# A GELU MLP's forward and backward on one core: part of the gate's arithmetic moved to GpSimd, and the first loads in another order

## The chip, the cores and the metric

One core of a Trainium2 chip runs the whole program. The metric is its device time in microseconds; three runs of the kernel before took 275.57, 275.65 and 275.70 us. Engines are named as in the profile: PE multiplies matrices, DVE, ACT and POOL (GpSimd) work element by element, SP issues DMAs, as ACT and POOL do too.

## The reference

```
h   = gelu(x @ w1 + b1)          # tanh form; x: 2048 x 448, w1: 448 x 1792
out = h @ w2 + b2                # w2: 1792 x 448
grads of x, w1, b1, w2, b2 from grad_out (2048 x 448)
```

All tensors are bf16. With v = x @ w1 + b1 the backward pass needs gelu'(v) times q, where q = grad_out @ w2 transposed; that product, gh, gives the gradients of x, w1 and b1, and h with grad_out gives that of w2.

## The kernel before, in words

The 2048 rows are four blocks of 512, the 1792 features seven pairs of 128-wide tiles, so there are 28 steps g (block, pair), and features lie on the partitions. The order of every engine's work is the order of the source: the schedule is written by hand, and each engine runs its own instructions in that order, waiting on the others where data demand it.

What a step computes, for a tile pair of 128 x 1024:

- PE: `M1` (L218) multiplies w1 with x into PSUM tile u, six matmuls of depth 128; `rest` (L229) adds the two of depth 64 and opens q with its own two; `M4` (L242) finishes q with six. u and q have one PSUM buffer each.
- ACT, `act_first` (L248): two rows copy u plus b1 into V (f32, the L252 rows), a Square with a scale gives A (L253), Gelu gives h (L254). `act_second` (L271): tanh of Bt into t (L272).
- DVE, `dve_first` (L268): Bt = (A + 3c) * V, the cubic. `dve_second` (L275): p = (A + c) * h, the slope (L276); t + 1 (L277); p - 0.5 (L278); t = t * p (L279). `dve_gate` (L281): gh = (t + 1) * q, with q read from PSUM.

V, A and Bt have one buffer each, t and p two each, in turn by the parity of the step.

The main loop (L373 to L416) does, for step g: `rest` for u of step g + 1 and q of step g, `M4(g)`, the gate of g, `act_first` and `dve_first` of g + 1, tanh and `dve_second` of g + 1, then "pieces", matmuls of output rows: those of h with w2 give out (o-pieces; in steps 0 to 6 eight each, for feature tiles 2g and 2g + 1), those of gh with w1 transposed give the gradient of x. `M1(g + 2)` ends the step on PE. Step 0's first part is done ahead of the loop (L367 to L372), with four dummy matmuls inside step 0 (L381 to L384). At step 6 the pieces, with two matmuls that add b2, and two copies on ACT stand ahead of tanh.

Loads are issued ahead of the loop, nearly all on SP's queue (L170 to L205), plain ones for w1 (`load_w1`, by feature columns) and w2 (`load_w2`, by feature tiles), transposing ones for x, grad_out (`load_x`, `load_g`; gq is the transposed grad_out of a block), w2 and w1 (`load_w2T`, `load_w1T`; each w2T load is two DMAs, L155 and L156). A DMA waits for the landing of the DMA eight places before it, and for what its target's data demand. A matmul that reads a part of w2 waits for the load that last wrote that part.

After step 27 come the rest of the pieces and the gradients of w1 and w2 (L430 to L499), all on PE, with sums for b1 and b2 on DVE and POOL's all-reduce (L446, L457).

Of the kernel before, what the change touches and what calls it, by code (L numbers as in the profile page):

```python
# [8 lines left out]
ACT = mybir.ActivationFunctionType  # L9
ALU = mybir.AluOpType  # L10
# [4 lines left out]
GELU_C = math.sqrt(2.0 / math.pi)  # L15
# [3 lines left out]
def kernel(  # L19
# [15 lines left out]
    nc = tc.nc  # L35
    P = 128
    B, S, D = x.shape
    F = w1.shape[1]
    assert B == 1
    NS = S // P  # L40
    NF = F // P
# [8 lines left out]
    NPAIR = NF // 2  # L50
# [33 lines left out]
    T_flat = const.tile([P, 4 * 2 * SB], BF16, name="T")  # L84
# [4 lines left out]
    w1_sb = w1_flat.rearrange("p (k f) -> p k f", k=KD)  # L89
# [9 lines left out]
    def xq(b):  # L99
        o = (b % 2) * 2 * KD * SB  # L100
        return xg_flat[:, o:o + KD * SB].rearrange("p (k s) -> p k s", k=KD)
# [5 lines left out]
    def ring(t, n, g):  # L107
        o = (g % n) * 2 * SB
        return t[:, o:o + 2 * SB].rearrange("p (h s) -> p h s", h=2)

    def hT(g):
        return ring(hT_flat, HR, g)
# [4 lines left out]
    def V_of(g):  # L117
        return VA_flat[:, 0:2 * SB].rearrange("p (h s) -> p h s", h=2)

    def A_of(g):  # L120
        return VA_flat[:, 2 * SB:4 * SB].rearrange("p (h s) -> p h s", h=2)

    def B_of(g):
        return ring(B_flat, 1, g)

    def t_of(g):
        return ring(T_flat, 4, 2 * (g % 2))

    def p_of(g):
        return ring(T_flat, 4, 2 * (g % 2) + 1)  # L130

    ctx.enter_context(tc.manual_schedule())

# [3 lines left out]
    def load_x(b):  # L137
        rows = slice(b * SB, (b + 1) * SB)
        nc.sync.dma_start_transpose(out=xq(b)[:, 0:KF, :], in_=x2[rows, DL:D])
        nc.sync.dma_start_transpose(out=xq(b)[:, KF, :], in_=x2[rows, 0:P])  # L140
# [6 lines left out]
    def load_w1(eng, f0, f1):  # L147
        eng.dma_start(out=w1_sb[:, 0:KF, f0:f1], in_=w1[DL:D, f0:f1].rearrange("(k p) f -> p k f", p=P))
        eng.dma_start(out=w1_sb[0:DL, KF, f0:f1], in_=w1[0:DL, f0:f1])

    def load_w2(eng, t0, t1):
        eng.dma_start(out=w2_sb[:, t0:t1, :], in_=w2[t0 * P:t1 * P, :].rearrange("(t p) d -> p t d", p=P))

    def load_w2T(f0, f1):
        nc.sync.dma_start_transpose(out=w2T_sb[:, KF, f0:f1], in_=w2[f0:f1, DOV:D])  # L155
        nc.sync.dma_start_transpose(out=w2T_sb[:, 0:KF, f0:f1], in_=w2[f0:f1, 0:DM])  # L156
# [21 lines left out]
    pw = psum_a.tile([P, SB], F32, name="acc")  # L178
# [8 lines left out]
        nc.tensor.matmul(pw[:], lhsT=warm[:, 0:P], rhs=warm, start=True, stop=True)  # L187
    load_w2T(256, 512)
    load_w2(nc.sync, 2, 4)
    load_w1(nc.sync, 768, 1280)  # L190
    load_w2T(512, 768)
    load_w2(nc.sync, 4, 8)
    load_w2T(768, 1024)
    load_w1(nc.sync, 1280, F)
    load_w2T(1024, 1280)
    load_w2(nc.sync, 8, NF)
    load_w2T(1280, 1536)
# [10 lines left out]
    def blk(g):  # L208
        return divmod(g, NPAIR)

    def cols(g, h):
        c = g % NPAIR
        return slice((2 * c + h) * P, (2 * c + h + 1) * P)
# [4 lines left out]
    def M1(g):  # L218
        if g == 0:
            u_of[g] = [psum_a.tile([P, SB], F32, name="acc")[:] for h in range(2)]  # L220
        else:
            u = psum_u.tile([P, 2, SB], F32, name="u")
            u_of[g] = [u[:, h, :] for h in range(2)]
        for h in range(2):
            for kt in range(KF):
                nc.tensor.matmul(u_of[g][h], lhsT=w1_sb[:, kt, cols(g, h)], rhs=xq(g // NPAIR)[:, kt, :],  # L226
                                 start=(kt == 0), stop=False, skip_group_check=True)

    def rest(gu, gg):  # L229

        if gg is not None:
            q = psum_g.tile([P, 2, SB], F32, name="q")
            g_of[gg] = q
        for h in range(2):
            if gu is not None:
                nc.tensor.matmul(u_of[gu][h], lhsT=w1_sb[0:DL, KF, cols(gu, h)], rhs=xq(gu // NPAIR)[0:DL, KF, :],  # L236
                                 start=False, stop=True, tile_position=(0, 0), skip_group_check=True)
            if gg is not None:
                nc.tensor.matmul(q[:, h, :], lhsT=w2T_sb[DL:P, KF, cols(gg, h)], rhs=gq(gg // NPAIR)[DL:P, KF, :],
                                 start=True, stop=False, tile_position=(DL, 0), skip_group_check=True)  # L240

    def M4(g):  # L242
        for h in range(2):
            for kt in range(KF):
                nc.tensor.matmul(g_of[g][:, h, :], lhsT=w2T_sb[:, kt, cols(g, h)], rhs=gq(g // NPAIR)[:, kt, :],  # L245
                                 start=False, stop=(kt == KF - 1), skip_group_check=True)

    def act_first(g):  # L248
        u = u_of.pop(g)
        for h in range(2):  # L250
            ft = 2 * (g % NPAIR) + h
            nc.scalar.activation(out=V_of(g)[:, h, :], in_=u[h], func=ACT.Identity, bias=b1_col[:, ft:ft + 1])  # L252
        nc.scalar.activation(out=A_of(g), in_=V_of(g), func=ACT.Square, scale=math.sqrt(3.0 * GELU_C * GELU_A))  # L253
        nc.scalar.activation(out=hT(g), in_=V_of(g), func=ACT.Gelu_apprx_tanh)  # L254

    def first_step(g):
# [8 lines left out]
                                           in1=V_of(g)[:, h, :], op0=ALU.add, op1=ALU.mult)  # L265
        nc.scalar.activation(out=hT(g), in_=V_of(g), func=ACT.Gelu_apprx_tanh)  # L266

    def dve_first(g):  # L268
        nc.vector.scalar_tensor_tensor(out=B_of(g), in0=A_of(g), scalar=3.0 * GELU_C, in1=V_of(g), op0=ALU.add, op1=ALU.mult)  # L269

    def act_second(g):  # L271
        nc.scalar.activation(out=t_of(g), in_=B_of(g), func=ACT.Tanh, scale=-1.0 / 3.0)  # L272


    def dve_second(g):  # L275
        nc.vector.scalar_tensor_tensor(out=p_of(g), in0=A_of(g), scalar=GELU_C, in1=hT(g), op0=ALU.add, op1=ALU.mult)  # L276
        nc.vector.tensor_scalar(out=t_of(g), in0=t_of(g), scalar1=1.0, scalar2=None, op0=ALU.add)  # L277
        nc.vector.tensor_scalar(out=p_of(g), in0=p_of(g), scalar1=-0.5, scalar2=None, op0=ALU.add)  # L278
        nc.vector.tensor_tensor(out=t_of(g), in0=t_of(g), in1=p_of(g), op=ALU.mult)  # L279

    def dve_gate(g):  # L281
        nc.vector.scalar_tensor_tensor(out=ghT(g), in0=t_of(g), scalar=1.0, in1=g_of.pop(g)[:], op0=ALU.add, op1=ALU.mult)  # L282

    def store_h(g):
        b, c = blk(g)
        nc.gpsimd.dma_start(out=hT_dram_v[:, 2 * c:2 * c + 2, b * SB:(b + 1) * SB], in_=hT(g))  # L286
# [50 lines left out]
    def run_pieces(units):  # L337
        for un in units:
            if un.piece():
                full.append(un)  # L340

    def flush(by_act=None):
        for un in [un for un in full if by_act in (None, un.by_act)]:
            full.remove(un)
            evict(un)
# [22 lines left out]
    rest(0, None)  # L368
    first_step(0)
    act_second(0)  # L370
    dve_second(0)
    M1(1)  # L372
    for g in range(NSTEP):  # L373
        b, c = blk(g)
        pieces = [U[k] for k in seq[b] for _ in range(NF)]
        n = len(pieces)
        own = pieces[n * c // NPAIR:n * (c + 1) // NPAIR]
        grown = [U[k] for k in grow[b] for _ in range(2)]
        nxt = g + 1 if g + 1 < NSTEP else None
        rest(nxt, g)  # L380
        if g == 0:  # L381

            for i in range(4):
                nc.tensor.matmul(pw[:], lhsT=w1_sb[:, 0, 0:P], rhs=xq(0)[:, 0, :], start=True, stop=True)  # L384
        M4(g)
        flush(False)
        dve_gate(g)
        if nxt is not None:
            act_first(nxt)
        flush(True)  # L390
        if nxt is not None:
            dve_first(nxt)
        last = b == 0 and c == NPAIR - 1
        if last:
            run_pieces(grown + own)
            flush(True)
        if nxt is not None:
            act_second(nxt)
            dve_second(nxt)
        if g == NPAIR:  # L400
            run_pieces(grown)
            M1(g + 2)
            run_pieces(own)
        elif not last:
            run_pieces(grown + own)
        if g != NPAIR and g + 2 < NSTEP:
            M1(g + 2)
        for _ in range(2):
            if g >= NPAIR - 1 and stored < g:
                store_h(stored)  # L410
                stored += 1
        if c == 2 and 0 < b < NB - 1:
            load_x(b + 1)
            load_g(b + 1)
        for t in turns.get(g, []):
            turn_gh(*t)  # L416
# [45 lines left out]
    for t0, t1 in ((0, 4), (4, HT)):  # L462
        n = (t1 - t0) * P
        for h in range(2):
            a0, a1 = t0 + h * HT, t1 + h * HT
            cs = slice(a0 * P, a1 * P)
            for kt in range(KF):
                ps = psum_a.tile([P, SB], F32, name="acc")
                psv = ps[:, 0:n].rearrange("p (t f) -> p t f", f=P)
                for st in range(NS):  # L470
                    nc.tensor.matmul(psv, lhsT=x_all[:, st, kt * P:(kt + 1) * P], rhs=gh_rows(st, a0, a1),  # L471
                                     start=(st == 0), stop=(st == NS - 1))
# [3 lines left out]
        for st in range(NS):  # L476
            for h in range(2):
                psv = ps[h * DL:(h + 1) * DL, 0:n].rearrange("p (t f) -> p t f", f=P)
                nc.tensor.matmul(psv, lhsT=x_all[:, st, KF * P:D], rhs=gh_rows(st, t0 + h * HT, t1 + h * HT),  # L479
                                 start=(st == 0), stop=(st == NS - 1), tile_position=(0, h * DL), skip_group_check=True)  # L480
        nc.scalar.copy(out=gw1_rem[:, t0 * P:t1 * P], in_=ps[:, 0:n])
        for h in range(2):
            nc.scalar.dma_start(out=out_2[KF * P:D, (t0 + h * HT) * P:(t1 + h * HT) * P],
                                in_=gw1_rem[h * DL:(h + 1) * DL, t0 * P:t1 * P])
# [45 lines left out]
```

## Time and profile before

| what | us |
|---|---|
| median of three runs | 275.65 |
| the profiled execution | 275.59 |
| its span in the profile | 273.8 |
| PE busy | 267.6 |
| DVE busy | 189.3 |
| ACT busy | 143.7 |
| POOL busy | 54.6 |
| step 3 on PE, first matmul of q to that of step 4 | 4.75 |

The profile is of one execution. Its busy lines give each engine's time at work; matmuls overlap, so that one row is longer than the distance to the next. A row of the timeline reads: start, length, engine, line, operation, what it writes and reads, shape, and in brackets the idle time before it and what ended that. A row of the DMA view reads: tiles, issuing queue, size, and the time from issue to landing. A row of the waits reads: who waited, for whom, the total, how often, the longest. Between the span and the device time lie 1.8 us of start and end that no row shows.

### The profile page before, as it was taken

The page shows a single profiled execution, that of the slowest core. Times are in us where ns is not written, and L with a number is a line of the kernel's source. Part 1 is how long each engine was busy: PE and PEld are TensorE (multiplying, and loading weights), DVE is VectorE, ACT ScalarE, POOL GpSimd, SP SyncE. Part 2 cuts the span into 40 slices and gives each one's busy share as a digit, 9 for nine tenths or more (in the row PEclk, how much of TensorE's full clock was granted, in tenths as well). Part 3 has the DMA queues.
Part 4 walks back from the last instruction along what each step waited for, and adds up shares of the span by engine and source line. Part 5 has one row for each costly group of instructions (what it writes and reads, how often), then busy time and mean ns, then how long its engine had stood idle before and what let it go on. Part 6 is the DMA issues. An engine that isn't in the chain of part 4 may idle for free.

```text
span 273.8 us, 3596 instructions
## 1 busy us (share of the span) xinstructions
PE 267.6 (98%) x1406; PEld 123.7 (45%) x1406; DVE 189.3 (69%) x218; ACT 143.7 (52%) x188; POOL 54.6 (20%) x57
## 2 busy tenths in 40 slices
PE   7899999999999999999999999999999999999995
PEld 3343434443444344444444445554445655555552
DVE  0799999999999999999888871139999970000000
ACT  2878879788888778887777740011111221112111
POOL 6000002730301403033031135111700019400000
PEclk9999999999999999999999999999999999999999
DMA  7878979999999928055534339999999931101111
GB/s 164 172 190 193 213 117 170 274 317 246 199 242 203 249 58 163 24 154 122 138 113 79 110 105 217 325 335 241 165 201 273 225 100 57 44 9 50 50 51 35
DMA packets 101379, 43.78 MB, mean 160 GB/s; under 512 B 90353, under 2 KB 97905, under 8 KB 101362
## 3 DMA queue, kind: packets, MB, share of 16 engines
q1 hardware_dynamic: 94272, 26.68, 51.6%
q0 software_dynamic: 4544, 14.92, 16.9%
q10 hardware_dynamic: 2546, 1.95, 2.5%
q8 instruction: 11, 0.18, 0.3%
q14 instruction: 6, 0.05, 0.1%
HBM read 7.00 MB, written 14.23 MB: 78 GB/s over the span
## 4 chain that ended last, share of the span: by engine, by line
PE 82%; DVE 12%; ACT 2%; DMA 2%; issue 1%; DVEq 0%
PE acc L313 27%; PE acc L490 16%; PE acc L471 13%; PE q L245 10%; PE u L226 9%; PE u L236 4%; DVE Bt L269 3%; DVE T L276 3%; DVE ghT_h L282 3%; PE acc L479 2%; DMA xg_h<-in_x_dram 2%; DVE T L279 2%; DVE T L277 1%; DVE T L278 1%; ACT VA L252 1%
## 5 line engine op out<-in xcount | busy, mean ns | idle before, releaser
L313 PE MATMUL acc<-w_gw,hT_h 128*128 128x448 bf16 x224 | 46.3, 352 | 0.2 <-ACT VA L252 0.2
L313 PE MATMUL acc<-w1T_gw,ghT_h 128*128 128x448 bf16 x224 | 45.1, 352 | 0.0
L245 PE MATMUL q<-xg_h,w2T_g 128*128 128x512 bf16 x168 | 41.1, 381 | 0.0
L252 ACT ACTIVATE VA<-u,b_col 128x512 f32<-128x512 f32 x54 | 34.0, 679 | 13.5 <-PE u L236 12.9
L226 PE MATMUL u<-xg_h,w_x 128*128 128x512 bf16 x162 | 39.4, 379 | 0.8 <-DMA w_x<-in_w_dram 0.4
L282 DVE SCALAR_TENSOR_TENSOR ghT_h<-T,q 128x1024 bf16<-128x1024 bf16 x28 | 34.2, 1221 | 8.4 <-PE q L245 7.0
L272 ACT ACTIVATE T<-Bt 128x1024 bf16<-128x1024 f32 x28 | 29.6, 1056 | 13.9 <-DVE Bt L269 13.8
L471 PE MATMUL acc<-gh_nat,w_x 128*128 128x512 bf16 (+1 forms) x192 | 36.7, 353 | 0.0
L276 DVE SCALAR_TENSOR_TENSOR T<-VA,hT_h 128x1024 bf16<-128x1024 f32 x28 | 34.1, 1219 | 0.2 <-ACT hT_h L266 0.2
L269 DVE SCALAR_TENSOR_TENSOR Bt<-VA 128x1024 f32<-128x1024 f32 x27 | 32.9, 1219 | 0.0
L313 PEld LDWEIGHTS <-hT_h 128*128 128x128 bf16 x224 | 21.9, 98 | 22.0 <-issue 0.5
L313 PEld LDWEIGHTS <-ghT_h 128*128 128x128 bf16 x224 | 21.9, 98 | 20.9
L456 DVE TENSOR_TENSOR VA<-VA,gh_nat 128x1792 f32<-128x1792 f32 x14 | 30.0, 2142 | 0.5
L253 ACT ACTIVATE VA<-VA 128x1024 f32<-128x1024 f32 x27 | 28.5, 1057 | 0.9
L254 ACT ACTIVATE hT_h<-VA 128x1024 bf16<-128x1024 f32 x27 | 28.1, 1040 | 0.0
L471 PEld LDWEIGHTS <-w_x 128*128 128x128 bf16 x192 | 18.7, 98 | 17.8 <-issue 0.4
L245 PEld LDWEIGHTS <-w2T_g 128*128 128x128 bf16 x168 | 14.2, 97 | 24.9 <-issue 11.4
L226 PEld LDWEIGHTS <-w_x 128*128 128x128 bf16 x168 | 16.3, 98 | 20.0 <-DMA w_x<-in_w_dram 1.4
L492 ACT CAST w_gw<-acc 128x448 bf16<-128x448 f32 x13 | 6.9, 532 | 32.6 <-PE acc L490 32.6
L333 POOL DMA_DIRECT2D out_dram<-io_o x8 | 5.8, 727 | 90.3 <-DVE io_o L329 48.6
L473 ACT CAST w1T_gw<-acc 128x512 bf16<-128x512 f32 (+1 forms) x12 | 6.3, 532 | 30.1 <-PE acc L471 24.2
L286 POOL DMA_DIRECT2D hT_dram<-hT_h x28 | 20.3, 728 | 1.9 <-DMA out_dram<-io_o 1.9
(60 smaller groups left out, 234.6 us busy)
## 6 DMA issues: line engine op xcount, KB each, us to landing
hT_dram<-hT_h POOLq DMA_DIRECT2D x28, 256.0 KB, 4.5
out_dram<-io_o POOLq DMA_DIRECT2D x8, 224.0 KB, 5.0
out_dram<-io_g POOLq DMA_DIRECT2D x8, 224.0 KB, 3.6
w_x<-in_x_dram POOLq DMA_DIRECT2D x1, 1792.0 KB, 10.8
w2T_g<-in_grad_out_dram POOLq DMA_DIRECT2D x1, 1792.0 KB, 14.7
out_dram<-w_gw SPq DMA_DIRECT2D x4, 336.0 KB, 2.4
w_x<-in_w_dram SPq DMA_DIRECT2D x2, 384.0 KB, 4.0
out_dram<-w1T_gw ACTq DMA_DIRECT2D x2, 384.0 KB, 5.4
```

The lines of the kernel that those rows point to most:

```text
L226: nc.tensor.matmul(u_of[g][h], lhsT=w1_sb[:, kt, cols(g, h)], rhs=xq(g // NPAIR)[:, kt, :], start=(kt == 0), stop=False, skip_group_check= ...
L245: nc.tensor.matmul(g_of[g][:, h, :], lhsT=w2T_sb[:, kt, cols(g, h)], rhs=gq(g // NPAIR)[:, kt, :], start=False, stop=(kt == KF - 1), skip_ ...
L252: nc.scalar.activation(out=V_of(g)[:, h, :], in_=u[h], func=ACT.Identity, bias=b1_col[:, ft:ft + 1])
L253: nc.scalar.activation(out=A_of(g), in_=V_of(g), func=ACT.Square, scale=math.sqrt(3.0 * GELU_C * GELU_A))
L269: nc.vector.scalar_tensor_tensor(out=B_of(g), in0=A_of(g), scalar=3.0 * GELU_C, in1=V_of(g), op0=ALU.add, op1=ALU.mult)
L272: nc.scalar.activation(out=t_of(g), in_=B_of(g), func=ACT.Tanh, scale=-1.0 / 3.0)
L276: nc.vector.scalar_tensor_tensor(out=p_of(g), in0=A_of(g), scalar=GELU_C, in1=hT(g), op0=ALU.add, op1=ALU.mult)
L282: nc.vector.scalar_tensor_tensor(out=ghT(g), in0=t_of(g), scalar=1.0, in1=g_of.pop(g)[:], op0=ALU.add, op1=ALU.mult)
L313: nc.tensor.matmul(self.ps[:, 0:D], lhsT=lhsT, rhs=rhs, start=(ft == 0), stop=(ft == NF - 1 and not bias))
L456: nc.vector.tensor_tensor(out=gsb_v, in0=gsb_v, in1=gh_rows(st, 0, NF), op=ALU.add)
L471: nc.tensor.matmul(psv, lhsT=x_all[:, st, kt * P:(kt + 1) * P], rhs=gh_rows(st, a0, a1), start=(st == 0), stop=(st == NS - 1))
L490: nc.tensor.matmul(ps[:, 0:D], lhsT=h_blk[ft][:, st, :], rhs=g_all[:, st, :], start=(st == 0), stop=(st == NS - 1))
```

## The change

For steps 1 to 7 POOL computes A + c into p (bf16), issued right ahead of the cubic, and DVE multiplies p by h in bf16 in place of its row with f32 operands. The cubic and the tanh of these steps are done by halves (128 x 512). t + 1 comes behind p - 0.5. p has one buffer in all steps. The dummy matmuls are three instead of four and stand ahead of step 0's `rest`. Of the loads, w1 is cut at column 1024 instead of 1280, w2 at tiles 6 and 8 with the cuts in another place of the queue; the line that loads w2's tiles 8 to 13 stays where it was, behind a new one that loads 6 to 13.

```diff
     def p_of(g):
-        return ring(T_flat, 4, 2 * (g % 2) + 1)
+        return ring(T_flat, 4, 1)
...
-    load_w1(nc.sync, 768, 1280)
+    load_w1(nc.sync, 768, 1024)
     load_w2T(512, 768)
-    load_w2(nc.sync, 4, 8)
+    load_w2(nc.sync, 4, 6)
+    load_w1(nc.sync, 1024, F)
     load_w2T(768, 1024)
-    load_w1(nc.sync, 1280, F)
+    load_w2(nc.sync, 6, NF)
     load_w2T(1024, 1280)
     load_w2(nc.sync, 8, NF)
     load_w2T(1280, 1536)
...
+    def by_pool(g):
+        return 0 < g <= NPAIR
+    def halves(g):
+        return ((0, 1), (1, 2)) if by_pool(g) else ((0, 2),)
+    def pool_slope(g):
+        nc.gpsimd.tensor_scalar(out=p_of(g), in0=A_of(g), scalar1=GELU_C, scalar2=None, op0=ALU.add)
     def dve_first(g):
-        nc.vector.scalar_tensor_tensor(out=B_of(g), in0=A_of(g), scalar=3.0 * GELU_C, in1=V_of(g), op0=ALU.add, op1=ALU.mult)
+        for h0, h1 in halves(g):
+            nc.vector.scalar_tensor_tensor(out=B_of(g)[:, h0:h1, :], in0=A_of(g)[:, h0:h1, :], scalar=3.0 * GELU_C,
+                                           in1=V_of(g)[:, h0:h1, :], op0=ALU.add, op1=ALU.mult)
     def act_second(g):
-        nc.scalar.activation(out=t_of(g), in_=B_of(g), func=ACT.Tanh, scale=-1.0 / 3.0)
+        for h0, h1 in halves(g):
+            nc.scalar.activation(out=t_of(g)[:, h0:h1, :], in_=B_of(g)[:, h0:h1, :], func=ACT.Tanh, scale=-1.0 / 3.0)
     def dve_second(g):
-        nc.vector.scalar_tensor_tensor(out=p_of(g), in0=A_of(g), scalar=GELU_C, in1=hT(g), op0=ALU.add, op1=ALU.mult)
-        nc.vector.tensor_scalar(out=t_of(g), in0=t_of(g), scalar1=1.0, scalar2=None, op0=ALU.add)
+        def add_t():
+            nc.vector.tensor_scalar(out=t_of(g), in0=t_of(g), scalar1=1.0, scalar2=None, op0=ALU.add)
+        if by_pool(g):
+            nc.vector.tensor_tensor(out=p_of(g), in0=p_of(g), in1=hT(g), op=ALU.mult)
+        else:
+            nc.vector.scalar_tensor_tensor(out=p_of(g), in0=A_of(g), scalar=GELU_C, in1=hT(g), op0=ALU.add, op1=ALU.mult)
+            add_t()
         nc.vector.tensor_scalar(out=p_of(g), in0=p_of(g), scalar1=-0.5, scalar2=None, op0=ALU.add)
+        if by_pool(g):
+            add_t()
         nc.vector.tensor_tensor(out=t_of(g), in0=t_of(g), in1=p_of(g), op=ALU.mult)
...
     M1(1)
+    for i in range(3):
+        nc.tensor.matmul(pw[:], lhsT=w1_sb[:, 0, 0:P], rhs=xq(0)[:, 0, :], start=True, stop=True)
     for g in range(NSTEP):
...
         rest(nxt, g)
-        if g == 0:
-            for i in range(4):
-                nc.tensor.matmul(pw[:], lhsT=w1_sb[:, 0, 0:P], rhs=xq(0)[:, 0, :], start=True, stop=True)
         M4(g)
         flush(False)
         dve_gate(g)
...
         if nxt is not None:
+            if by_pool(nxt):
+                pool_slope(nxt)
             dve_first(nxt)
```

## The prediction

> **What bounds the kernel now.** I read the page's busy table and chain first.
>
> ```profile
> PE 267.6 (98%) x1406; PEld 123.7 (45%) x1406; DVE 189.3 (69%) x218; ACT 143.7 (52%) x188; POOL 54.6 (20%) x57
> PE 82%; DVE 12%; ACT 2%; DMA 2%; issue 1%; DVEq 0%
> ```
>
> PE is busy for 267.6 of 273.8 us, so all that any change of DVE can win is in PE's few gaps. The chain names DVE for 12%; in order of time those rows lie between 14.5 and 47.7 us, steps 0 to 7. After that the chain is PE row behind PE row to 270.6, so what PE loses or wins before 50 us reaches the end undiminished. Where PE stands still is in its own waits:
>
> ```profile
> PE q L239 <- DMA w2T_g<-in_w_dram: 0.5, 1, 0.5
> PE u L226 <- DMA w_x<-in_w_dram: 0.4, 1, 0.4
> PE u L226 <- ACT VA L252: 0.4, 1, 0.4
> PE acc L313 <- ACT VA L252: 0.2, 1, 0.2
> ```
>
> (Waited for, total, times, longest.) The last line is misnamed: in the timeline these pieces start at 23.07, and the w2 load of four tiles, issued at 18.15, lands 4.9 later, at 23.05. So loads cause three of the four. The third, at 48.46, is the DVE and ACT chain: M1(9) waits until V(8) has emptied u.
>
> The timeline gives one step of DVE (start, length):
>
> ```profile
> 24.65 1.22 DVE L269 SCALAR_TENSOR_TENSOR Bt<-VA 128x1024 f32<-128x1024 f32 x1
> 25.78 1.22 DVE L276 SCALAR_TENSOR_TENSOR T<-VA,hT_h 128x1024 bf16<-128x1024 f32 x1
> 26.99 0.43 DVE L277 TENSOR_SCALAR T<-T 128x1024 bf16<-128x1024 bf16 x1
> 27.33 0.42 DVE L278 TENSOR_SCALAR T<-T 128x1024 bf16<-128x1024 bf16 x1
> 27.79 0.69 DVE L279 TENSOR_TENSOR T<-T 128x1024 bf16<-128x1024 bf16 x1
> 28.58 1.22 DVE L282 SCALAR_TENSOR_TENSOR ghT_h<-T,q 128x1024 bf16<-128x1024 bf16 x1
> ```
>
> From 24.65 to the next cubic at 29.72 is 5.07 us, without a gap. PE needs 4.75 for the same step (25.97 to 30.72, q's first matmul to the next). PE starts ahead and loses 0.32 per step of its lead; the lead ends at 48.46. That is what the change is aimed at: some 0.5 us there.
>
> **Part 1, arithmetic.** DVE loses a 1.14 row (start to start, L276) and gets a product of bf16 operands, 0.69 by L279: 5.07 - 1.14 + 0.69 = 4.62. The cubic by halves costs about 0.1 more (two 128x512 rows at L264 take 1.29 together, one 128x1024 row 1.22): 4.7. Tanh by halves adds 0.1 to ACT (L262: two halves 1.15, L253: 1.06), which has 0.82 idle per step. The reordered +1 costs nothing: the row is the same. The slope's one buffer instead of two costs nothing either: POOL's row waits for the step before's last product (28.48 in this step), and Square, on which it waits too, ends at 29.20.
>
> POOL's new row, 128x1024 f32 to bf16, has no counterpart. From below: its memset L168 wrote 3072 elements in 2.66, so 0.87 for 1024. From above: its all-reduce of 128x448 f32, by what it took from DVE:
>
> ```profile
> 192.07 4.58 POOL L446 PARTITION_ALL_REDUCE T<-Bt  x1 [4.04 <-DVE Bt L445]
> 191.89 2.02 DVE L454 TENSOR_TENSOR VA<-gh_nat 128x1792 f32<-128x1792 bf16 x1
> 193.94 3.66 DVE L456 TENSOR_TENSOR VA<-VA,gh_nat 128x1792 f32<-128x1792 f32 x1
> ```
>
> The row at 193.94 takes 3.66 where its thirteen sisters take 2.03: 1.63 lost to a POOL row that reads 448 elements, 3.7 us for 1024. I take 1.1, near the memset, since both stream element by element, and 1.2 with the start. The Trainium skill (GPSIMD Engine Reference, 3.1) gives 1.03 cycles per element at 1.2 GHz for simple bodies, 0.88 us as an estimate.
>
> The same pair shows a thing against the change: a DVE row with two SBUF inputs stood still beside a reading POOL. The gate has one operand in PSUM; the cubic behind it has two in SBUF. POOL starts when Square ends (24.13 in this step), the gate ends at 24.73, so with 1.2 POOL is still reading until 25.3 and the cubic waits 0.6. A step is then Square's end, POOL 1.2, cubic 1.27, second tanh half 0.6, two V rows 1.28, Square 1.04: 5.4, not 4.7. The Trainium skill (SBUF — State Buffer, Who interferes with whom) says that such an instruction fully blocks until the other ends; the 1.63 agrees. By it a step is 5.4; without it 4.7, below PE's 4.75. Which of them holds matters only if DVE is late at all, and below it is not.
>
> **Part 2, the fillers.** Four dummy matmuls, 0.87 (11.00 to 11.87), leave the front of M4(0); three stand where PE waits for w2T anyway (the 0.5 above). But M4(0) needs w2T's other part, issued at 8.17; L156's rows land 3.0 to 4.6 after issue, 3.2 in the median, so at about 11.4. Gain 0.4 of the 0.87 (from 0 to 0.87).
>
> **Part 3, the loads.** Here is the price. SP issues in order; a DMA waits for the one eight places before it. From 18.15 on the old row of loads was w2[4:8], w2T, w1 of 512 columns, w2T, w2[8:14]. Now it is w2[4:6], w1[1024:1792], w2T, w2[6:14], w2T, and w2[8:14] **again**: the old line was left. That second load overwrites what the first one wrote, so the program order gives it a wait for the first one's landing, and SP stands there with everything behind it.
>
> ```profile
> w_gw<-in_w_dram SPq DMA_DIRECT2D x2, 224.0 KB, 3.0
> w_gw<-in_w_dram SPq DMA_DIRECT2D x1, 448.0 KB, 4.9
> w_gw<-in_w_dram SPq DMA_DIRECT2D x1, 672.0 KB, 5.5
> ```
>
> (Issue to landing.) Step by step:
> - w2[4:6], 224 KB: 18.15 + 3.0 = 21.2. The 0.4 at 23.07 (PE could have gone on at 22.67) is gone. PE is 0.8 ahead.
> - w1[1024:1792], 576 KB, issued at 18.8: between 4.9 and 5.5, so 24.0. M1(4), ready at 24.58 - 0.8 = 23.8, loses 0.2 (0 to 0.5).
> - w2[6:14], 896 KB, is issued after 0.6 + 0.6 + 0.55 + 1.25 + 1.3 to 2.1 (rows of SP for w2, two of w1, two of w2T): 22.5 to 23.3. From the three sizes 896 KB takes 6.1 (last slope), 6.75 (mean slope) to 7.4; I take 7.0, since the w1 load before it is the larger now. It lands at 29.9 (28.6 to 30.7). Before, w2[6:8] had been there at 23.05.
> - Step 3's eight o-pieces read tiles 6 and 7. PE reaches them at 27.82 - 0.6 = 27.2, and waits until **29.9: 2.7 lost** (1.4 to 3.5). M1(5) stands behind them.
> - w2[8:14] again: issued at 29.95, lands 5.2 later at 35.15. Step 4's pieces, ready at 29.9 + 4.75 = 34.65, lose 0.5.
> - PE then goes 4.75 per step: step 6's pieces at 44.65, 1.89 of them with the bias, M1(8) 1.39, first matmuls of step 7 at 47.93, M4(7) at 48.5. In the old run 45.88.
> - gq(1), which M4(7) reads, was issued 14.5 after w2[8:14] (25.89 to 40.41) and landed 4.9 later, at 45.3, only 0.6 ahead of its use. Now 29.95 + 19.4 = 49.4; if SP's ten rows run at their shortest, 12, and land 4.5 behind, 46.5. I take 49.0: 0.5 more.
> - M1(9): 49.0 + 1.30 + 0.76 = 51.06, against 48.46. V(8) must be copied by then. With POOL at p us, cubic(5) starts at 35.75 + p, each step takes 4.2 + p, V(8) ends 3.15 behind cubic(7): 47.3 + 3p, so 50.9 for p = 1.2. In time, barely; the old 0.5 there is gone because PE is late, not because DVE is quick.
>
> Sum: 51.06 - 48.46 = +2.6 on the profiled execution's 275.59 (which lies 0.06 under the median): **278.2**. Nothing later gives it back, since PE has no wait behind 48.46.
>
> **Rivals.**
> - *POOL's lock binds.* From p = 1.25 on 47.3 + 3p is later than PE; 1.65 gives +1.2, 279.4; 2.0 gives +2.2, 280.4; at 3.8 the chain alone, 8 us per step over six steps from 17.4, ends at 69 and gives 296. For it: the 3.66 row. Against the far end: the memset's rate. Chance 0.2, mostly 279 to 281.
> - *PE's clock falls in the stall.* It is granted 1.00 in every window of the trace; a stall of 2.7 us has no counterpart after 6 us. If the following 3.4 us of work went at half speed, 1.7 would be lost, of which the waits at 35.15 and 49.0 hide 0.5 to 1: 279.2. The Trainium skill (TensorE: Matmul & The Clock Gate, Part 1) sets the drop behind an idle window of about 3.4 us; 2.7 would stay below it. Chance 0.05.
> - *Faster: loads arrive in time.* If 896 KB landed within 4.3 us, by 27.2, and gq(1) by 44.5, the three gaps (0.4, 0.4, 0.5) are won: 274.3. It decides at 27.2. Against: 448 KB took 4.9. Chance 0.06. Half way, a landing near 27.9 to 28.6 and gq(1) early, is no change: 0.05.
> - The forecast, 277.2 to 279.2: 0.64.
>
> Anything within 0.2% (0.55 us) is what a measurement here can't tell from no change. Range: the forecast's, downward to a landing at 28.6 with gq(1) early (+1.2), upward to p = 2: 276.8 to 280.5. Faster 0.06, same 0.05, slower 0.89.
>
> **What would show it.** Right: PE's waits name w_gw before step 3's pieces with 2 to 3 us, SP's row for w2[8:14] starts when the load before it lands, and DVE has idle time in steps 4 to 7. The cubic's first half starts when POOL's row ends, later than the gate's end. Wrong: PE has no gap near 27 us (the load was quick), or M1 rows wait for ACT in steps 2 to 6 (POOL is slow), or POOL's row runs beside an undisturbed cubic (no lock). Wrong in size if w2[6:14] lands outside 28.6 to 30.7.

## The result and the profile after

The changed kernel takes **277.95 us** (median of four runs, 277.82 to 278.03) against 275.61 for the kernel before on the same chip: ratio 1.0085 [1.0067, 1.0102], slower. The prediction was 278.2, within 276.8 to 280.5. The profiled execution took 278.03 with a span of 276.3, 2.5 more than before. Ratios leave out executions that ran throughout at a lower granted clock, as one of no_pool's did (351.03 at 0.755).

The page's busy line, the chain, and then four rows of the waits (who waited, for whom, total, times, longest):

```profile
PE 268.3 (97%) x1405; PEld 124.1 (45%) x1405; DVE 187.2 (68%) x225; ACT 145.0 (52%) x195; POOL 73.8 (27%) x64
PE 81%; SPq 8%; DMA 2%; DVE 2%; ACT 2%; POOL 2%; issue 1%; ACTq 0%; DVEq 0%
```

```profile
PE q L246 <- DMA w2T_g<-in_w_dram: 1.4, 2, 1.0
PE acc L335 <- DMA w_gw<-in_w_dram: 1.3, 1, 1.3
PE u L227 <- ACT VA L253: 0.3, 1, 0.3
DVE T L294 <- POOL T L278: 3.9, 7, 0.6
```

DVE is busy 2 us less and POOL 19 us more; the chain now names SP's load issues with 8%, and POOL with 2%. PE waits three times for loads (0.34 at M4(0), 1.03 at M4(2), 1.30 at step 3's pieces), and at M1(9) it **still waits for V(8)**. DVE waits for POOL in all seven steps. One step of DVE, with POOL's row in its place, from the timeline:

```profile
24.25 1.22 DVE L304 SCALAR_TENSOR_TENSOR ghT_h<-T,q 128x1024 bf16<-128x1024 bf16 x1
24.52 2.77 POOL L278 TENSOR_SCALAR T<-VA 128x1024 bf16<-128x1024 f32 x1 [2.63 <-ACT VA L254]
25.39 1.32 DVE L282 SCALAR_TENSOR_TENSOR Bt<-VA 128x512 f32<-128x512 f32 x2
27.33 0.69 DVE L294 TENSOR_TENSOR T<-T,hT_h 128x1024 bf16<-128x1024 bf16 x1 [0.62 <-POOL T L278]
28.05 0.43 DVE L298 TENSOR_SCALAR T<-T 128x1024 bf16<-128x1024 bf16 x1
28.40 0.42 DVE L292 TENSOR_SCALAR T<-T 128x1024 bf16<-128x1024 bf16 x1
28.85 0.69 DVE L301 TENSOR_TENSOR T<-T 128x1024 bf16<-128x1024 bf16 x1
29.65 1.22 DVE L304 SCALAR_TENSOR_TENSOR ghT_h<-T,q 128x1024 bf16<-128x1024 bf16 x1
29.75 2.77 POOL L278 TENSOR_SCALAR T<-VA 128x1024 bf16<-128x1024 f32 x1 [2.46 <-ACT VA L254]
```

POOL's row is 2.77 us long, and the product behind the cubic stands until it ends. The cubic stands beside it almost undisturbed (1.32). From gate to gate it is 5.40; the gates of steps 0 to 6 start at 13.35, 19.05, 24.25, 29.65, 34.87, 40.67 and 45.91, in the mean 5.4 apart where the old step was 5.07. DVE has less work in a step, and its step became longer. The chain that closes runs over two steps: cubic (25.39), tanh, V, Square of the next step (28.61), POOL's row (29.75 to 32.52), product, constants, product, gate (34.87), cubic (36.01): 10.62 us, 5.31 a step. The next two steps take 11.03: the cubic at 36.01 is held 0.44, and ACT's V(5) waits 0.32 for u, which PE finishes late behind its stall at step 3.

Where PE's rows start against before (after minus before):

| PE's row | before | after | difference |
|---|---|---|---|
| M4(0) | 11.87 | 11.24 | -0.63 |
| M4(2), behind a w2T load | 21.36 | 21.94 | +0.58 |
| step 2's o-pieces | 23.07 | 23.25 | +0.18 |
| step 3's o-pieces, behind w2[6:14] | 27.82 | 29.46 | +1.64 |
| `rest` of step 7 | 45.34 | 47.05 | +1.71 |
| M1(9), behind V(8) | 48.46 | 50.20 | +1.74 |
| step 8's `rest` | 51.36 | 53.35 | +1.99 |
| last matmuls' copy on ACT, L498 and L521 | 270.62 | 272.65 | +2.03 |

So most of the loss (1.99 of 2.5) is there before 54 us, as forecast. But two causes arrive at M1(9) together: PE's stalls for loads, and a late V(8). The experiments separate them.

### The profile page after: what moved, and what is told of

The parts are those of the page before. It is cut to its first block, busy times and chain, and to the rows that moved or that the text cites. A ratio compares the mean times of both kernels' runs of the same rounds, so it can differ in the third digit from the quotient of the medians.

```text
span 276.3 us, 3633 instructions
## 1 busy us (share of the span) xinstructions
PE 268.3 (97%) x1405; PEld 124.1 (45%) x1405; DVE 187.2 (68%) x225; ACT 145.0 (52%) x195; POOL 73.8 (27%) x64
## 4 chain that ended last, share of the span: by engine, by line
PE 81%; SPq 8%; DMA 2%; DVE 2%; ACT 2%; POOL 2%; issue 1%; ACTq 0%; DVEq 0%
PE acc L335 27%; PE acc L513 15%; PE acc L494 13%; PE q L246 10%; PE u L227 9%; PE u L237 4%; PE acc L502 2%; DMA w_gw<-in_w_dram 2%; SPq L155 2%; POOL T L278 2%; SPq L156 2%; ACT VA L253 1%; ACT VA L254 1%; SPq L145 1%; SPq L152 1%
## 5 line engine op out<-in xcount | busy, mean ns | idle before, releaser
L287 ACT ACTIVATE T<-Bt 128x1024 bf16<-128x1024 f32 (+1 forms) x35 | 30.8, 886 | 13.9 <-DVE Bt L282 13.8
L282 DVE SCALAR_TENSOR_TENSOR Bt<-VA 128x1024 f32<-128x1024 f32 (+1 forms) x34 | 34.1, 1020 | 0.0
L278 POOL TENSOR_SCALAR T<-VA 128x1024 bf16<-128x1024 f32 x7 | 19.4, 2775 | 24.7 <-ACT VA L254 24.7
L296 DVE SCALAR_TENSOR_TENSOR T<-VA,hT_h 128x1024 bf16<-128x1024 f32 x21 | 25.6, 1218 | 0.2 <-ACT hT_h L267 0.2
L355 POOL DMA_DIRECT2D out_dram<-io_g x8 | 5.8, 727 | 56.5 <-ACT io_g L349 50.9
```

The source lines that it names most:

```text
L282: nc.vector.scalar_tensor_tensor(out=B_of(g)[:, h0:h1, :], in0=A_of(g)[:, h0:h1, :], scalar=3.0 * GELU_C, in1=V_of(g)[:, h0:h1, :], op0=AL ...
L287: nc.scalar.activation(out=t_of(g)[:, h0:h1, :], in_=B_of(g)[:, h0:h1, :], func=ACT.Tanh, scale=-1.0 / 3.0)
```

## The experiments

### Loads or arithmetic

Four kernels take the change apart. **loads_mended** is the changed kernel with the new w2 load ended at tile 8; **loads_old** has the old loads; **loads_alone** is the kernel before with the new loads; **no_second_load** drops the load that was left in place.

```diff
# loads_mended, against the changed kernel
-    load_w2(nc.sync, 6, NF)
+    load_w2(nc.sync, 6, 8)
```

> The changed kernel, but the load that repeats itself is cut: w2[6:8] instead of w2[6:14] ahead of w2[8:14]. Theory A (the 2.4 us come from the loads): PE's gap of 1.3 us before step 3's pieces goes, PE stays ahead, 276.4 or less. Rival B (POOL's row of 2.77 us has become the bound: in the changed kernel DVE goes 5.3 us per step, gate to gate, instead of 5.07): PE only waits later, at M1(9), for V(8), which ends near 49.8 instead of 50.2; 277.3 to 277.7.

```diff
# loads_old, against the changed kernel
-    load_w1(nc.sync, 768, 1024)
+    load_w1(nc.sync, 768, 1280)
-    load_w2(nc.sync, 4, 6)
-    load_w1(nc.sync, 1024, F)
+    load_w2(nc.sync, 4, 8)
-    load_w2(nc.sync, 6, NF)
+    load_w1(nc.sync, 1280, F)
```

> The changed kernel with all loads in the old order; the POOL row, the halves and the fillers stay. A: as before or slightly faster, 275.3. B: the step of 5.3 us alone sets the end of V(8), 277.1 to 277.4.

```diff
# loads_alone, against the kernel before
-    load_w1(nc.sync, 768, 1280)
+    load_w1(nc.sync, 768, 1024)
-    load_w2(nc.sync, 4, 8)
+    load_w2(nc.sync, 4, 6)
+    load_w1(nc.sync, 1024, F)
-    load_w1(nc.sync, 1280, F)
+    load_w2(nc.sync, 6, NF)
```

> The kernel before with the new row of loads and nothing else (four fillers, no POOL, no halves). A: PE waits for w2[6:14] until about 29.4 before step 3's pieces and keeps 1 to 1.6 us of it: 276.6 to 277.3. B: DVE's step is 5.07 and the loads cost nothing in the end, 275.6.

```diff
# no_second_load, against the changed kernel
-    load_w2(nc.sync, 8, NF)
```

> The changed kernel without its second load of w2[8:14]; w2[6:14] is one load still. The prediction's step that SP stands for the first landing and that this costs 1.0 us (0.5 at step 4's pieces, 0.5 at M4(7)): 276.9 or less. What the trace of the changed kernel says, that PE waited for neither: 277.6 to 277.95, SP's queue 2.5 us earlier with no effect on PE.

| kernel | median | before | ratio | M1(9) at | PE's waits from 9 us on |
|---|---|---|---|---|---|
| loads_mended | 277.38 | 275.82 | 1.0056 [1.0043, 1.0069] | 49.84 | V(8) 0.3, w2 0.3, w2T 0.2 |
| loads_old | 277.26 | 275.82 | 1.0053 [1.0041, 1.0065] | 49.98 | w2 1.2, w2T 0.3, V(8) 0.3 |
| loads_alone | 276.76 | 275.82 | 1.0034 [1.0022, 1.0047] | 49.24 | w2 1.7, no V(8) |
| no_second_load | 277.84 | 275.82 | 1.0084 [1.0057, 1.0112] | 50.09 | w2 1.3, w2T 0.4, V(8) 0.3 |

What follows. The arithmetic without the new loads costs 1.4 us, the loads without the arithmetic 0.9. By the medians the two add up: both together cost 2.3. On PE they hide one another in part: the last copy on ACT comes 1.69 later than before in loads_old, 0.79 in loads_alone and 2.03 in the changed kernel. M1(9) of the changed kernel and of the three others with the arithmetic lies at 49.8 to 50.2 and waits for V(8), however long the loads stall; the stall itself reaches V(8) a little, by ACT's wait of 0.32, and the changed kernel's M1(9) is 0.36 behind that of loads_mended. The second load costs nothing that these runs show: without it M1(9) is 0.11 earlier and the median the same (six runs from 277.28 to 280.28), against the 1.0 (0.5 and 0.5) that the prediction gave it.

### Is it POOL?

**no_pool**: the mended loads, the new place of three fillers, one buffer for p, and no step with POOL or halves.

```diff
     def by_pool(g):
-        return 0 < g <= NPAIR
+        return False
```

> The changed kernel with the mended loads (w2[6:8], no repeat) and with no step given to POOL, so DVE's rows are those of the kernel before; one slope buffer and the three fillers stay. If POOL's row is what made loads_mended late (C): the step of DVE is 5.07 again, M1(9) near 48.5, 275.3 to 275.9. If something else of the change costs (D: fillers, loads, one slope buffer): 276.5 or more.

275.71 against 275.88, ratio 0.9999 [0.9988, 1.001]. All of the arithmetic's loss is POOL and the halves, which were not parted here; fillers and mended loads by themselves give nothing that can be measured.

**row_out** asks what the aim was worth: the kernel before without DVE's row t + 1 in steps 1 to 7.

```diff
-        nc.vector.tensor_scalar(out=t_of(g), in0=t_of(g), scalar1=1.0, scalar2=None, op0=ALU.add)
+        if not 0 < g <= NPAIR:
+            nc.vector.tensor_scalar(out=t_of(g), in0=t_of(g), scalar1=1.0, scalar2=None, op0=ALU.add)
```

> The kernel before with one thing taken out: DVE's row t + 1 (0.43 us by its row) is left out in steps 1 to 7, so the gradients of these steps are not the reference's; loads, fillers, POOL as before. It measures what a shorter DVE chain is worth when nothing is put on POOL for it. Theory (the chain of DVE, 5.07 per step, costs PE only the 0.4 us at M1(9), and the loads' waits of 0.5, 0.4 and 0.2 are other matters): a step of DVE becomes 4.65, below PE's 4.75, the wait at M1(9) goes, the others stay: 275.1 to 275.3 against 275.6, ratio 0.998 to 0.999. Rival (the chain's lateness also holds PE in places that the waits don't name, 0.3 per step): 274 or less. Rival (another wait, a load, takes its place at M1(9)): no change, 275.6.

275.48 against 275.74, ratio 0.9992 [0.9981, 1.0002]; the interval holds no change. The trace shows the mechanism: M1(9) starts without a wait.

```profile
47.24 0.92 PE L314 MATMUL acc<-w_gw,hT_h 128*128 128x448 bf16 x4
48.00 1.46 PE L226 MATMUL u<-xg_h,w_x 128*128 128x512 bf16 x6
```

48.00 against 48.46: a quicker DVE, for nothing, is worth 0.46 us on PE in these two traces. That is the most the arithmetic could have won with the old loads, and POOL cost three times as much.

### Length or lock?

POOL's row can hurt by its length (the product waits for it) or by holding DVE's rows. **pool_probe** prices both: no_pool's kernel with one POOL row that nobody reads in each of steps 8 to 27, by turns of five kinds (add on f32, add on bf16, memset, add on 512, copy).

```diff
+    def probe(g):
+        o = ring(T_flat, 4, 3)
+        k = g % 5
+        if k == 0:
+            nc.gpsimd.tensor_scalar(out=o, in0=A_of(g), scalar1=GELU_C, scalar2=None, op0=ALU.add)
...
+        else:
+            nc.gpsimd.tensor_copy(out=o, in_=A_of(g))
...
+            if nxt > NPAIR:
+                probe(nxt)
```

> no_pool's kernel, where in steps 8 to 27 POOL does one more row whose result nobody reads, behind Square, in turn: add f32 to bf16 1024, add bf16 to bf16 1024, memset bf16 1024, add f32 to bf16 512, copy f32 to bf16 1024. Lock as the prediction had it (a reading row holds DVE's cubic, which has two SBUF operands, until it ends): cubics of 1.22 become 2 to 4 us beside the adds and the copy, 1.22 beside the memset. What the changed kernel's trace suggests (only the first 0.9 us of a 2.77 row holds it): 2.0 to 2.1 beside 1024 elements whatever the row's length, 1.6 beside 512. Prices: the f32 add 2.77, the memset 0.9.

Groups of POOL's rows (busy in total, mean ns of one, idle time before), each kind four times:

```profile
L281 POOL TENSOR_SCALAR T<-VA 128x1024 bf16<-128x1024 f32 x4 | 11.4, 2843 | 5.6 <-ACT VA L254 5.5
L283 POOL TENSOR_SCALAR T<-hT_h 128x1024 bf16<-128x1024 bf16 x4 | 11.1, 2787 | 0.1
L287 POOL TENSOR_SCALAR T<-VA 128x512 bf16<-128x512 f32 x4 | 6.0, 1500 | 10.0 <-PE u L237 7.3 <-ACT VA L254 2.6
L289 POOL CAST T<-VA 128x1024 bf16<-128x1024 f32 x4 | 4.7, 1185 | 6.1 <-ACT VA L254 6.1
```

An add costs 2.8 us whatever its input's type, a copy 1.2 and, undisturbed, 1.03. The lock, from its timeline:

```profile
65.76 2.77 POOL L281 TENSOR_SCALAR T<-VA 128x1024 bf16<-128x1024 f32 x1 [1.17 <-ACT VA L254]
67.14 1.22 DVE L296 SCALAR_TENSOR_TENSOR Bt<-VA 128x1024 f32<-128x1024 f32 x1
...
70.02 2.79 POOL L283 TENSOR_SCALAR T<-hT_h 128x1024 bf16<-128x1024 bf16 x1
71.29 1.81 DVE L312 TENSOR_SCALAR T<-T 128x1024 bf16<-128x1024 bf16 x1
...
98.14 2.80 POOL L281 TENSOR_SCALAR T<-VA 128x1024 bf16<-128x1024 f32 x1
98.19 2.09 DVE L310 SCALAR_TENSOR_TENSOR T<-VA,hT_h 128x1024 bf16<-128x1024 f32 x1
```

The cubic at 67.14 begins 1.38 after POOL's add, in the middle of it, and takes its usual 1.22. The row at 98.19 begins 0.05 after an add and takes 2.09, 0.87 more; one that began 0.27 after took 1.84. So an add holds a DVE row with two SBUF operands only in its first **0.9 us**, in which it seems to read, and not for its 2.77. A bf16 row of 0.42 is another case: the one at 71.29, begun 1.27 after a bf16 add, takes 1.81 and ends 0.29 behind the add. It need not be held to the end: the one at 129.30, begun 0.40 after an f32 add, takes 1.19 and ends 1.45 ahead of the add's end. What lets it go stays open.

In the changed kernel the cubic starts 0.87 behind POOL's row in the step shown and loses next to nothing; only in steps 1 and 5, where it started 0.61 and 0.46 behind, it took 1.60 and 1.73 instead of 1.29. It is the length that counts there. Then a shorter row ought to win; three kernels tried that with mended loads, two of them also behind the change's own.

**copy_for_add**: POOL copies A in place of adding c to it.

```diff
-        nc.gpsimd.tensor_scalar(out=p_of(g), in0=A_of(g), scalar1=GELU_C, scalar2=None, op0=ALU.add)
+        nc.gpsimd.tensor_copy(out=p_of(g), in_=A_of(g))
```

> loads_mended's kernel with POOL copying A to bf16 instead of adding the constant (the constant is left out of the slope in steps 1 to 7); the copy measured 1.03 us where the add takes 2.77, and both hold a cubic for 0.9. C (the length of POOL's row binds, by the product that waits for it): DVE falls to 4.7 us per step, below PE's 4.75, and PE has no wait for V(8): 274.3 to 274.9, faster than before. If the lock's 0.9 is what binds, it stays with loads_mended, 277.4.

277.21 against 275.8, ratio 1.0049 [1.003, 1.0068]: a miss. The timeline:

```profile
23.43 1.22 DVE L304 SCALAR_TENSOR_TENSOR ghT_h<-T,q 128x1024 bf16<-128x1024 bf16 x1
24.57 1.84 DVE L282 SCALAR_TENSOR_TENSOR Bt<-VA 128x512 f32<-128x512 f32 x2
26.34 0.68 DVE L294 TENSOR_TENSOR T<-T,hT_h 128x1024 bf16<-128x1024 bf16 x1
```

POOL's copy starts at 24.23 and takes 1.04. The product waits for nothing now, so the gate comes sooner, the cubic meets the copy's read and loses 0.55. The loop that closes is now cubic, tanh, V, Square, the copy's read, cubic: 5.21 a step, still more than 5.07. The length had been hiding the lock.

**pool_halved**: Square, POOL's row and the product by halves, +1 between them, so that each half goes on at once. **pool_halved_after_loads**: the same behind the change's own loads.

```diff
-        nc.gpsimd.tensor_scalar(out=p_of(g), in0=A_of(g), scalar1=GELU_C, scalar2=None, op0=ALU.add)
+        for h in range(2):
+            nc.gpsimd.tensor_scalar(out=p_of(g)[:, h, :], in0=A_of(g)[:, h, :], scalar1=GELU_C, scalar2=None, op0=ALU.add)
```

> The mended loads; Square, POOL's row and the bf16 product are done by halves, +1 between the two products. C, with the two-step chain cubic, tanh, V, Square, POOL, product, gate: it shortens by half a Square and half a product and +1 per two steps, to about 4.8 us per step instead of 5.3; V(8) no longer ends last, 274.6 to 275.4, faster than the kernel before. If POOL's price lies in a start cost of each row (two rows then take much more than one of 2.77): slower than loads_mended's 277.4.

> The same halves with the changed kernel's own loads, repeat included. If loads and POOL's chain hide one another (either alone late by 1 to 1.5 us, both by 2.3): with the chain short the loads show alone, as in loads_alone, +0.6 to +1.2 on the kernel before, 276.4 to 277.0. If they add: 1.0 below the changed kernel or less gain.

279.66 and 279.56 against 275.88, ratios 1.0133 [1.0118, 1.0149] and 1.0138 [1.0121, 1.0155]: worse than the change, a miss. In the timeline of the first:

```profile
24.33 3.12 POOL L281 TENSOR_SCALAR T<-VA 128x512 bf16<-128x512 f32 x2 [2.47 <-DVE T L305]
25.41 1.70 DVE L285 SCALAR_TENSOR_TENSOR Bt<-VA 128x512 f32<-128x512 f32 x2
27.81 0.43 DVE L295 TENSOR_SCALAR T<-T 128x1024 bf16<-128x1024 bf16 x1 [0.36 <-ACT T L290]
```

Two rows read at two times, and the second read meets the cubic's second half: 1.70 instead of 1.3, and 3.12 instead of 2.77. Then +1, which stands between the two products, waits 0.36 for the second half of tanh. A step is 5.59. Another cause is mixed in: from step 2 on POOL's row waits for the last product of the step before (DVE T L305), since p has one buffer, and Square's first half was done about 0.5 sooner. With two buffers POOL's reads would come earlier; that was not tried. The pair also shows the overlap: behind a later chain the loads' stall (1.4 in the second kernel) costs nothing.

**half_share**: POOL adds c for one half only, DVE does the other as before, cubic and tanh whole. **half_share_after_loads**: the same behind the change's own loads.

```diff
-        nc.gpsimd.tensor_scalar(out=p_of(g), in0=A_of(g), scalar1=GELU_C, scalar2=None, op0=ALU.add)
+        nc.gpsimd.tensor_scalar(out=p_of(g)[:, 1, :], in0=A_of(g)[:, 1, :], scalar1=GELU_C, scalar2=None, op0=ALU.add)
...
-            nc.vector.tensor_tensor(out=p_of(g), in0=p_of(g), in1=hT(g), op=ALU.mult)
+            nc.vector.scalar_tensor_tensor(out=p_of(g)[:, 0, :], in0=A_of(g)[:, 0, :], scalar=GELU_C,
+                                           in1=hT(g)[:, 0, :], op0=ALU.add, op1=ALU.mult)
+            nc.vector.tensor_tensor(out=p_of(g)[:, 1, :], in0=p_of(g)[:, 1, :], in1=hT(g)[:, 1, :], op=ALU.mult)
```

> Mended loads; POOL adds the constant for the second half of the slope alone (512 elements, 1.49 us), DVE does the first half with its old f32 row and the second as a bf16 product; cubic and tanh whole again. POOL is done before DVE asks: a step of 5.07 - 1.14 + 0.6 + 0.4 = 4.9 us, 0.15 behind PE, and PE's lead of some 2 us lasts beyond step 8. C: 274.3 to 275.2, faster than both kernels. If any POOL row beside these steps costs DVE more than it takes off: 275.9 or more.

> half_share with the changed kernel's own loads, repeat included. With the chain short the loads show alone: PE waits 1 to 2 us before step 3's pieces and keeps it, 1.2 to 2 above half_share. If the loads are hidden as in pool_halved_after_loads (279.56 against 279.66), no difference to half_share.

half_share: 276.38 against 275.8, ratio 1.0025 [1.0014, 1.0036]; the least bad, and a miss too. A step is 5.15: two rows of 512 take 0.60 and 0.45 where one of 1024 took 1.14, and +1 waits 0.2 for tanh. With the change's loads: 277.37, ratio 1.0069 [1.0046, 1.0093], seven runs from 276.56 to 277.74 and three at 279.2 to 279.4. The traced one is of the three. PE's timeline, and the same stretch in windows (busy of PE, PEld, DVE, ACT and POOL, granted clock, DMA share, GB/s):

```profile
29.86 3.15 PE L336 MATMUL acc<-w_gw,hT_h 128*128 128x448 bf16 x8 [2.27 <-DMA w_gw<-in_w_dram]
32.80 1.65 PE L227 MATMUL u<-xg_h,w_x 128*128 128x512 bf16 x6
```

```profile
27.00:30.00 3.00, 0.73 (x4) 0.29 (x3) 2.75 (x5) 2.92 (x5) 0.54 (x1) 0.96 1.11 287
30.00:32.00 2.00, 2.00 (x6) 0.76 (x5) 2.00 (x3) 1.14 (x2) 0.94 (x1) 0.50 0.54 107
32.00:34.00 2.00, 2.00 (x8) 0.84 (x7) 1.53 (x4) 0.23 (x1) 0.00 (x0) 0.70 1.27 326
34.00:36.00 2.00, 2.00 (x12) 0.62 (x10) 0.00 (x0) 0.91 (x2) 0.00 (x0) 1.00 1.17 235
```

Behind a stall of 2.27 us the granted clock is 0.50 (0.96 in the window from 27 to 30, 0.70 from 32 to 34, so some 3.4 us at half in all), and the pieces take 3.15 instead of 1.68, M1 1.65 instead of 1.46: 1.66 lost, three quarters of the 2.16 from the seven runs' median to the three's. The mean clock is 0.992 to 0.994 over the three runs and 0.998 or more over the seven; 0.994 stands also beside one of six runs of no_second_load (280.28) and one of five of pool_halved_after_loads (280.54), which have the same load of eight tiles and were not traced in those runs. That is the prediction's second rival, in another kernel than the one it was made for; in the changed kernel, whose stall is 1.3, every window's clock is 1.00.

## Why the prediction was right, and where not

The time came out 0.25 below the forecast, and most of it where forecast, but by another last wait: the prediction said that loads decide M1(9) and DVE's lateness is harmless. In the run V(8) decides it. That the sum came so near is in part luck: the loads, on which it rests, cost 0.9 by themselves (loads_alone) and not 2.6, and the arithmetic, which has no price in it, costs 1.4 by itself (loads_old). By terms of the sum, start to start on PE:

| term | predicted | measured |
|---|---|---|
| fillers moved | -0.4 | -0.63 |
| old wait for w2 at step 2 | -0.4 | -0.40 |
| w2T load before M4(2) | not named | +1.21 |
| w1 load | +0.2 | 0 |
| w2[6:14] before step 3's pieces | +2.7 | +1.46 |
| second w2 load, then gq(1) | +0.5, +0.5 | 0, 0 |
| q behind a late gate, steps 6 and 7 | not named | +0.19 |
| V(8)'s wait at M1(9) | -0.5 | -0.09 |
| behind M1(9) | 0 | +0.25, and some 0.4 behind the last matmul |

- **w2[6:14]** was right in mechanism: it landed at 29.43, predicted 29.9, and PE waits there. The term was mis-sized because PE came later: another load, w2T's second part, issued at 16.79 as before, landed at 21.89 and not at 19.90. Why it landed late stays open. It does not come with the new queue of loads as such: loads_alone and no_second_load issue the same loads up to there, and their M4(2) starts without that wait, at 21.07 and 21.16 (in copy_for_add and half_share it waits 0.37 and 0.59). It also costs little, since step 3's pieces start at 29.12 in both of them: w2[6:14] decides there, whenever PE comes.
- **The second load**: SP does stand from 26.44 to 29.43, as predicted. But the load landed after 4.3, at 33.74, ahead of the pieces (34.20), and gq(1) at 47.10 (predicted 49.0), ahead of M4(7) at 47.70. The step failed by 1.4 and 1.9 us of landing time.
- **POOL's row**, the step that failed: I took 1.1 (bounds 0.87 and 3.7), near the memset; it is 2.77. (The memset's 2.66 for 3072 elements make 0.89 for 1024, not 0.87.) A memset (0.97) and a copy (1.03) run near the rate that the memset's row showed, an add at less than half of it, so "both stream element by element" was no reason. The Trainium skill (GPSIMD Engine Reference, 3.1) gives 1.03 cycles per element for simple bodies, 0.88 us as an estimate: the copy, 1.03, comes near it; the add is three times as long.
- **The lock**: I let the cubic wait until POOL's row ends. It waits for the first 0.9 us of it. The row that I read for it, at 193.94, already said so: its 1.63 of standing end at 195.57, and POOL's row ends at 196.65. The Trainium skill (SBUF — State Buffer, Who interferes with whom) says such an instruction fully blocks until the other ends; the 1.22 cubic in the middle of POOL's 2.77 speaks against that. By my formula a p of 2.77 puts V(8)'s end at 47.3 + 3p = 55.6; it was at 50.15. A row too short and a lock too long offset each other. The first rival named this place, M1(9), and missed the means: it is the product's wait for POOL, not the cubic's. The sign that DVE would have idle time in steps 4 to 7 came true for the same reason, 0.48 to 0.62 ahead of each product there, and not because PE is late.
- **Behind M1(9)** the prediction saw nothing. Step 7's x-gradient pieces start 1.54 behind M1(9), before it was 1.29, right behind the first of DVE's late copies of the output (two from 51.07 on); in pool_halved, where the same distance is 1.64, PE's wait names that copy. In the traced execution the span ends 2.5 later, ACT's last copy 2.03. The other 0.4 lies behind that copy and does not go with the change: from ACT's last copy to the end it is 3.2 us before and in loads_old, 3.6 in the changed kernel and in loads_alone.
- **The clock**: the Trainium skill (TensorE: Matmul & The Clock Gate, Part 1) sets the drop behind an idle window of about 3.4 us, and I let a stall of 2.7 stay below it. Here 2.27 was enough, in the traced run at least. With the 2.7 that I forecast for step 3, that rival deserved more than 0.05.

No kernel here beats the one before. What stays open: whether ACT could write A and V in bf16 or otherwise take 0.4 us per step off DVE; it wasn't tried.

## What to carry to other kernels

Offloading a row pays only if the helper's latency fits between producer and consumer: here a 1.14 us row on DVE became a 2.77 us row on POOL that DVE waits for, inside a loop in which DVE had no gap. Ask first what the aim is worth by leaving the row out: 0.46 us. And when two late things meet at one wait, mending one can show less than it costs by itself (loads_mended's M1(9) is 0.36 earlier, loads_alone's 0.78 later than before); take the other away to price it.

## What the hardware showed beyond that

- POOL: an add of 128x1024 2.77 us from f32 or bf16, of 128x512 1.5, a copy 1.03, a memset 0.97.
- POOL's add holds a DVE row with two SBUF operands for its first 0.9 us (1024 elements: 2.09 instead of 1.22) or 0.5 (512 elements: a cubic at 115.81, begun with the add, took 1.72). Bf16 rows of 0.42 were held longer: two took 1.81 and 1.19, the first to the add's end.
- A stall of 2.27 us on PE was followed by some 3.4 us at half the clock; behind the stalls of 1.3 to 1.7 in the changed kernel and loads_alone the windows show 1.00.
